# A Fourier mixing and gated feed-forward kernel: the order of six matmuls in a step of the tensor engine

## The chip, the cores and the metric

The kernel runs on one core of a Trainium2 chip. The core has a tensor engine for matrix products (PE in the profile; its loads of weights are PEld), a vector engine (DVE), a scalar engine (ACT), a general engine (POOL) and an engine that mostly issues transfers (SP). Matrix products land in PSUM, which DVE and ACT read; everything else lies in SBUF or in the chip's memory. Each engine works through its own list of instructions in order and waits on semaphores for the others. The metric is the device time of one execution, in microseconds (us), as the median of the runs made.

## The reference

```python
def _attn_ref(x):                       # x: (8, 3008, 256)
    X = np.fft.fft(x, axis=1)
    X = np.fft.fft(X, axis=2)
    return X.real.astype(np.float32)

def _moe_ref(x, w_gate, w_val, w_out):  # 24064 tokens, d_model 256, d_ff 1536
    gate = np.maximum(x @ w_gate, 0.0)
    val = x @ w_val
    return (gate * val @ w_out).astype(np.float32)

def reference(...):
    x = _attn_ref(x).reshape(24064, 256)
    return _moe_ref(x, w_gate, w_val, w_out)
```

The input is mixed by a Fourier transform along the sequence and the features, of which the real part is kept. Each token then goes through a gate (with a relu), a value, their product and an output projection.

## The kernel before, in words

The sequence transform of length 3008 is taken as 94 x 32, in two stages of matrix products with a trip through the chip's memory between them. For each of the eight batches, `stage1` (eight pieces, matmuls of L117 and L121) makes the first stage. `shuffle_out` (L134) and `shuffle_in` (L140) write its result out and read it back in another layout, both issued by SP. `rotate` (L146, L147) mends one column, and `stage2` (L157, six pieces) makes the tiles `pq`, one for each of three blocks of a batch. The feature transform is folded into the weights: `wc`, `ws` and `wm` hold gate (index 0) and value (index 1) weights multiplied by cosines and sines. Before stage 1, POOL folds the input of a batch (L88 to L100), which SP (L73) and POOL itself (L76, a gather) have loaded.

The transform of a real input has a mirror symmetry, and the feed-forward uses it. A block's tile `pq` has a part 0 and a part 1. For 128 of the 1536 hidden units at a time, one step computes the gate `G` and the value `V` for 512 tokens as `wc` times part 0 plus `ws` times part 1 (the function `plus`). ACT takes the relu of `G` into `gs` (L349) and DVE multiplies it with `V` into the first half of `h` (L350). Then the function `minus` adds one more product, `wm` times part 1, into the same `G` and `V`, which turns them into the gate and value of the 512 mirrored tokens. Again ACT takes a relu (L360) and DVE a product (L362, into the second half of `h`, with the tokens turned round). So the matmul of `minus` into `G` must wait until the relu of `plus` has read `G`, and the matmul of `minus` into `V` until the product of `plus` has read `V`.

There are 8 x 3 x 12 = 288 steps. The kernel's order is written out by hand: instructions go to each engine in the order of the code. The main loop makes one turn for each step and twelve more. Turn t does `minus` of step t-1, `plus` of step t, then what the table `extra` holds for this turn (the pieces of the coming batch: `load_x`, `fold_all`, `stage1`, the two shuffles, `rotate`, `stage2`), and then `out_piece` of step t-12, eight matmuls with the output weights (L380). The first twelve turns have no output matmuls, and the last twelve have nothing else. Every third turn an output tile `po` is complete; it is copied by DVE (L384) and by ACT (L386) in turn, at the end of the turn that completes it, and after each copy by ACT four stores are issued on SP (L395 or L401). For the second batch, stage 1 falls in turns 16 to 23, the shuffles are issued in turn 24 and `rotate` stands in turn 28; for later batches eight turns of stage 1 end one turn before the shuffles, and `rotate` comes seven turns after these.

`G` and `V` have two PSUM buffers each, `gs` has four, `h` has 25.

Of the kernel before, what the change touches and what calls it, by code (L numbers as in the profile page):

```python
# [10 lines left out]
F32 = mybir.dt.float32  # L11
BF16 = mybir.dt.bfloat16
I32 = mybir.dt.int32
ALU = mybir.AluOpType
ACTF = mybir.ActivationFunctionType
# [10 lines left out]
def free(ap, offset, *dims):  # L26

    part = list(ap.ap[0])
    return bass.AP(ap.tensor, ap.offset + offset, [part] + [list(d) for d in dims])
# [12 lines left out]
def kernel(ctx: ExitStack, tc, x, w_gate, w_val, w_out, out):  # L42
# [3 lines left out]
    nc = tc.nc  # L46
    B, S, D = x.shape
    DF = w_gate.shape[1]
    NA, NB = 94, 32
# [125 lines left out]
    wc = [const.tile([128, DF], BF16, tag=f"wc{i}", name=f"wc{i}") for i in range(2)]  # L175
    ws = [const.tile([128, DF], BF16, tag=f"ws{i}", name=f"ws{i}") for i in range(2)]
    wm = [const.tile([128, DF], BF16, tag=f"wm{i}", name=f"wm{i}") for i in range(2)]
    wo = const.tile([128, NF, D], BF16, tag="wo")

    with tc.tile_pool(name="st", bufs=1, space=SB) as st, \  # L180
# [3 lines left out]
        for i, w in enumerate((w_gate, w_val)):  # L184
            t = st.tile([128, 2, DF], F32, tag=f"wst{i}", name=f"wst{i}")
# [122 lines left out]
        for n in range(DF // 512):  # L308
            for i in range(2):
                for cs in range(2):  # L310
                    ps = psw.tile([128, 512], F32, tag="w", name="psw")
                    for c in range(2):
                        nc.tensor.matmul(ps[:], lhsT=cd[:, c, cs, :], rhs=wst[i][:, c, n * 512:(n + 1) * 512],  # L313
                                         start=(c == 0), stop=(c == 1))
# [13 lines left out]
    gp = ctx.enter_context(tc.tile_pool(name="gp", bufs=4, space=SB))  # L328
    hp = ctx.enter_context(tc.tile_pool(name="hp", bufs=2 * NF + 1, space=SB))
    op = ctx.enter_context(tc.tile_pool(name="op", bufs=4, space=SB))  # L330
    psg = ctx.enter_context(tc.tile_pool(name="psg", bufs=2, space=PS))
    psv = ctx.enter_context(tc.tile_pool(name="psv", bufs=2, space=PS))
    pso = ctx.enter_context(tc.tile_pool(name="pso", bufs=2, space=PS))

    steps = [(b, blk, f) for b in range(B) for blk in range(NBLK) for f in range(NF)]
    ht = {}

    def plus(b, blk, f):
        pq = pqt[b, blk]
        fs = slice(f * 128, (f + 1) * 128)  # L340
        h = hp.tile([128, 2, 512], BF16, tag="h", name="h")
        G = psg.tile([128, 512], F32, tag="g", name="G")
        V = psv.tile([128, 512], F32, tag="v", name="V")
        ht[b, blk, f] = (h, G, V)
        for i, acc in enumerate((G, V)):
            nc.tensor.matmul(acc[:], lhsT=wc[i][:, fs], rhs=pq[:, 0, :], start=True, stop=False)  # L346
            nc.tensor.matmul(acc[:], lhsT=ws[i][:, fs], rhs=pq[:, 1, :], start=False, stop=True)  # L347
        gs = gp.tile([128, 512], F32, tag="gs", name="gs")
        nc.scalar.activation(gs[:], G[:], ACTF.Relu)  # L349
        nc.vector.tensor_tensor(h[:, 0, :], gs[:], V[:], op=ALU.mult)  # L350

    def minus(b, blk, f):
        pq = pqt[b, blk]
        fs = slice(f * 128, (f + 1) * 128)
        h, G, V = ht[b, blk, f]
        for i, acc in enumerate((G, V)):
            nc.tensor.matmul(acc[:], lhsT=wm[i][:, fs], rhs=pq[:, 1, :], start=False, stop=True,  # L357
                             skip_group_check=True)
        gs = gp.tile([128, 512], F32, tag="gs", name="gs")
        nc.scalar.activation(gs[:], G[:], ACTF.Relu)  # L360

        nc.vector.tensor_tensor(free(h[:], 512 + NB - 1, [NB, 16], [-1, NB]),  # L362
                                gs[:].rearrange("p (a k) -> p a k", k=NB),
                                V[:].rearrange("p (a k) -> p a k", k=NB), op=ALU.mult)
        ht[b, blk, f] = h

    state = {}

    def out_piece(b, blk, f):

        for k in range(8 * f, 8 * f + 8):
            gi, ff = divmod(k, NF)
            sg, s = divmod(gi, 4)
            g = 3 - s if sg else s
            if s == 0 and ff == 0:
                state["os"] = op.tile([128, 4, D], F32, tag="os", name="os")
            if s % 2 == 0 and ff == 0:
                state["po"] = pso.tile([128, 2, D], F32, tag="o", name="po")
            po, os_ = state["po"], state["os"]
            nc.tensor.matmul(po[:, s % 2, :], lhsT=ht[b, blk, ff][:, sg, g * 128:(g + 1) * 128],  # L380
                             rhs=wo[:, ff, :], start=(ff == 0), stop=(ff == NF - 1))
            if s % 2 == 1 and ff == NF - 1:
                if s == 1:
                    nc.vector.tensor_copy(os_[:, s - 1:s + 1, :], po[:])  # L384
                else:
                    nc.scalar.copy(os_[:, s - 1:s + 1, :], po[:])  # L386
            if s == 3 and ff == NF - 1:
                store(b, blk, sg, os_)
# [35 lines left out]

    n = len(steps)
    for t in range(n + NF):
        if 0 < t <= n:
            minus(*steps[t - 1])
        if t < n:
            plus(*steps[t])  # L430
        for fn in extra.get(t, ()):
            fn()
        if t >= NF:
            b, blk, f = steps[t - NF]
            out_piece(b, blk, f)
# [30 lines left out]
```

## Time and profile before

| | us |
|---|---|
| median of 3 runs | 752.11 |
| lowest and highest | 751.88, 752.16 |
| the profiled execution | 752.15 |
| its span in the profile | 750.4 |
| first matmul of the main loop starts (in the span) | 70.87 |
| first output matmul starts | 98.42 |
| last matmul that isn't an output matmul starts | 734.21 |

How to read it: the profiled execution is one run with the hardware profiler on, and its span goes from the first to the last instruction that the profile shows, so that some 1.75 us of its time lie around the span. Times within the profile are counted from the span's start. The page of the profile gives each engine's busy time, the granted clock of the tensor engine in slices, the groups of instructions by line of the code, and which instruction ended each wait. The timeline gives single instructions: start, duration, engine, line, operation, tiles written and read, and in brackets the idle time of that engine before the instruction with the engine and line that ended it. The end of a matmul is modelled, and matmuls overlap: of two that follow each other without a wait, the second starts before the row of the first has ended. Buffer numbers stand behind the names of tiles where several tiles have one name.

### The profile page before, as it was taken

Reading aid. Unit: us, or ns where it says so; the run is one execution under the profiler, and the core shown is the slowest. Engines: PE = TensorE matmul, PEld = TensorE weight load, DVE = VectorE, ACT = ScalarE, POOL = GpSimd, SP = SyncE. Lnnn points to the kernel's source line nnn. Section 1 sums busy time; section 2 is a strip of 40 time slices with the busy share of each in tenths; the row PEclk is TensorE's granted clock in tenths of the full one; section 3 lists DMA queues with packets and bytes.
Section 4 is the critical chain, followed back from the end, with each engine's and each line's share of the span. In section 5 each row is a group of like instructions: output and inputs, shape, how many; then the busy total and the mean of one; then the engine's idle time right before and its main releaser. Section 6 shows DMA issues by size and latency. Waiting matters only on the chain.

```text
span 750.4 us, 12199 instructions
## 1 busy us (share of the span) xinstructions
PE 692.4 (92%) x4432; PEld 430.6 (57%) x4432; DVE 481.0 (64%) x747; ACT 408.3 (54%) x701; POOL 221.6 (30%) x116
## 2 busy tenths in 40 slices
PE   0178799999999999999999999999999999999997
PEld 0033256566666666666666666666666666666565
DVE  6613666666666766766666767666667667666672
ACT  2114556556565656556565655556565655555551
POOL 2837739102920086004900094005800000000000
PEclk9999999999999999999999999999999999999999
DMA  9466253616342534116241454135221141211213
GB/s 195 165 164 113 62 112 93 157 29 151 104 111 57 115 112 113 56 41 172 71 135 33 116 139 111 29 82 143 59 55 29 32 136 28 53 33 28 55 29 82
DMA packets 26971, 67.61 MB, mean 90 GB/s; under 512 B 3856, under 2 KB 17680, under 8 KB 24720
## 3 DMA queue, kind: packets, MB, share of 16 engines
q1 hardware_dynamic: 24340, 51.84, 26.6%
q0 software_dynamic: 2448, 13.37, 8.2%
q10 hardware_dynamic: 124, 1.64, 0.9%
q8 instruction: 34, 0.56, 0.3%
q14 instruction: 25, 0.20, 0.1%
HBM read 36.68 MB, written 30.93 MB: 90 GB/s over the span
## 4 chain that ended last, share of the span: by engine, by line
PE 82%; DVE 6%; ACT 4%; POOL 3%; issue 3%; DMA 1%; ACTq 0%; POOLq 0%; DVEq 0%
PE po L380 30%; PE V L357 10%; PE G L347 7%; PE G L346 7%; PE V L347 7%; PE V L346 7%; PE G L357 7%; DVE h L350 4%; PE psw L313 3%; ACT gs L360 2%; ACT gs L349 1%; DVE h L362 1%; DMA t_969<-Td 1%; DMA Td<-t_719 1%; DVE q L37 0%
## 5 line engine op out<-in xcount | busy, mean ns | idle before, releaser
L362 DVE TENSOR_TENSOR h<-gs,V 128x512 bf16<-128x512 f32 x288 | 198.1, 688 | 203.4 <-ACT gs L360 148.6
L380 PE MATMUL po<-wo,h 128*128 128x256 bf16 x2304 | 296.8, 272 | 0.0
L360 ACT ACTIVATE gs<-G 128x512 f32<-128x512 f32 x288 | 172.2, 598 | 214.1 <-PE G L357 214.1
L380 PEld LDWEIGHTS <-h 128*128 128x128 bf16 x2304 | 222.7, 98 | 64.1 <-issue 2.0
L350 DVE TENSOR_TENSOR h<-gs,V 128x512 bf16<-128x512 f32 x288 | 197.8, 687 | 11.3 <-ACT gs L349 9.9
L349 ACT ACTIVATE gs<-G 128x512 f32<-128x512 f32 x288 | 172.3, 598 | 30.9 <-PE G L347 14.7
L88 POOL TENSOR_TENSOR xc<-xl,xh 94x3840 f32<-94x3840 f32 (+1 forms) x8 | 60.6, 7574 | 302.2 <-DMA xl<-in_x_dram 268.8
L357 PE MATMUL V<-pq,wm_92 128*128 128x512 bf16 x288 | 108.6, 377 | 6.3 <-DVE h L350 4.2
L357 PE MATMUL G<-pq,wm_91 128*128 128x512 bf16 x288 | 109.1, 379 | 3.1 <-ACT gs L349 3.1
L347 PE MATMUL V<-pq,ws_90 128*128 128x512 bf16 x288 | 109.2, 379 | 0.0
L346 PE MATMUL V<-pq,wc_88 128*128 128x512 bf16 x288 | 109.0, 378 | 0.0
L347 PE MATMUL G<-pq,ws_89 128*128 128x512 bf16 x288 | 108.9, 378 | 0.0
L346 PE MATMUL G<-pq,wc_87 128*128 128x512 bf16 x288 | 108.8, 378 | 0.0
L89 POOL TENSOR_TENSOR xl<-xl,xh 94x3840 f32<-94x3840 f32 (+1 forms) x8 | 60.6, 7578 | 0.6
L346 PEld LDWEIGHTS <-wc_87 128*128 128x128 bf16 x288 | 27.7, 96 | 54.5 <-issue 43.2
L347 PEld LDWEIGHTS <-ws_90 128*128 128x128 bf16 x288 | 28.0, 97 | 34.2
L386 ACT COPY os<-po 128x512 f32<-128x512 f32 x48 | 28.1, 586 | 35.6 <-PE po L380 35.6
L346 PEld LDWEIGHTS <-wc_88 128*128 128x128 bf16 x288 | 27.8, 97 | 34.3
L347 PEld LDWEIGHTS <-ws_89 128*128 128x128 bf16 x288 | 27.7, 96 | 34.2
L117 PEld LDWEIGHTS <-w_82 94*96 94x96 bf16 x120 | 15.7, 131 | 50.5 <-issue 28.1
L384 DVE COPY os<-po 128x512 f32<-128x512 f32 x48 | 33.0, 688 | 6.9 <-PE po L380 6.9
L357 PEld LDWEIGHTS <-wm_92 128*128 128x128 bf16 x288 | 28.2, 98 | 9.6 <-issue 6.5
(345 smaller groups left out, 346.8 us busy)
## 6 DMA issues: line engine op xcount, KB each, us to landing
out_dram<-os SPq DMA_DIRECT2D x176, 128.0 KB, 2.1
xl<-in_x_dram SPq DMA_DIRECT2D x7, 1360.0 KB, 9.8
xl<-in_x_dram SPq DMA_DIRECT2D x7, 238.0 KB
wst_103<-in_moe_w_gate_dram SPq DMA_DIRECT2D x2, 768.0 KB, 20.4
wst_106<-in_moe_w_val_dram SPq DMA_DIRECT2D x2, 768.0 KB, 23.7
out_dram<-os SPq DMA_DIRECT2D x16, 96.0 KB, 4.5
xl<-in_x_dram ACTq DMA_DIRECT2D x1, 1360.0 KB
Td<-t_256 SPq DMA_DIRECT2D x4, 192.0 KB, 9.2
```

Of the source, the lines that this page charges most:

```text
L88: eng.tensor_tensor(c1, x1, rev, op=ALU.subtract)
L89: eng.tensor_tensor(x1, x1, rev, op=ALU.add)
L346: nc.tensor.matmul(acc[:], lhsT=wc[i][:, fs], rhs=pq[:, 0, :], start=True, stop=False)
L347: nc.tensor.matmul(acc[:], lhsT=ws[i][:, fs], rhs=pq[:, 1, :], start=False, stop=True)
L349: nc.scalar.activation(gs[:], G[:], ACTF.Relu)
L350: nc.vector.tensor_tensor(h[:, 0, :], gs[:], V[:], op=ALU.mult)
L357: nc.tensor.matmul(acc[:], lhsT=wm[i][:, fs], rhs=pq[:, 1, :], start=False, stop=True, skip_group_check=True)
L360: nc.scalar.activation(gs[:], G[:], ACTF.Relu)
L362: nc.vector.tensor_tensor(free(h[:], 512 + NB - 1, [NB, 16], [-1, NB]), gs[:].rearrange("p (a k) -> p a k", k=NB), V[:].rearrange("p (a k) ...
L380: nc.tensor.matmul(po[:, s % 2, :], lhsT=ht[b, blk, ff][:, sg, g * 128:(g + 1) * 128], rhs=wo[:, ff, :], start=(ff == 0), stop=(ff == NF - 1))
L384: nc.vector.tensor_copy(os_[:, s - 1:s + 1, :], po[:])
L386: nc.scalar.copy(os_[:, s - 1:s + 1, :], po[:])
```

## The change

`plus` and `minus` get a further argument, 0 for the gate and 1 for the value, and do only that half. The main loop runs over it, so that a turn's matmuls come as: `minus` into G, `plus` into G (two), `minus` into V, `plus` into V (two). Before, both matmuls of `minus` came first.

```diff
-    def plus(b, blk, f):
+    def plus(b, blk, f, i):
...
-        for i, acc in enumerate((G, V)):
-            nc.tensor.matmul(acc[:], lhsT=wc[i][:, fs], rhs=pq[:, 0, :], start=True, stop=False)
-            nc.tensor.matmul(acc[:], lhsT=ws[i][:, fs], rhs=pq[:, 1, :], start=False, stop=True)
-        gs = gp.tile([128, 512], F32, tag="gs", name="gs")
-        nc.scalar.activation(gs[:], G[:], ACTF.Relu)
-        nc.vector.tensor_tensor(h[:, 0, :], gs[:], V[:], op=ALU.mult)
...
+        e = ht[b, blk, f]
+        nc.tensor.matmul(e[i][:], lhsT=wc[i][:, fs], rhs=pq[:, 0, :], start=True, stop=False)
+        nc.tensor.matmul(e[i][:], lhsT=ws[i][:, fs], rhs=pq[:, 1, :], start=False, stop=True)
+        if i == 0:
+            e["gs"] = gp.tile([128, 512], F32, tag="gs", name="gs")
+            nc.scalar.activation(e["gs"][:], e[0][:], ACTF.Relu)
+        else:
+            nc.vector.tensor_tensor(e["h"][:, 0, :], e["gs"][:], e[1][:], op=ALU.mult)
...
     for t in range(n + NF):
-        if 0 < t <= n:
-            minus(*steps[t - 1])
-        if t < n:
-            plus(*steps[t])
+        for i in range(2):
+            if 0 < t <= n:
+                minus(*steps[t - 1], i)
+            if t < n:
+                plus(*steps[t], i)
         for fn in extra.get(t, ()):
             fn()
```

`minus` is split in the same way: its one matmul by `i`, the relu with the gate, the product with the value. Each engine keeps the number of its instructions. ACT's and DVE's lists stay in their order (relu of `minus`, relu of `plus`; product of `minus`, product of `plus`), and so do the lists of SP and POOL. The change moves lines of the code: L346, L347 and L357 before are L347, L348 and L360 after; the relus L349 and L360 are L351 and L364, the products L350 and L362 are L353 and L367, the output matmuls L380 are L385.

The tensor engine's list at the first turn with a `minus` (turn 1; V_435 and G_434 are tiles of step 0, V_450 and G_449 before, V_448 and G_447 after, those of step 1; in brackets the semaphore that an instruction waits for, by the engine that raises it). Before:

```order
L357 LDWEIGHTS wm0_91
L357 MATMUL G_434<-pq_376,wm0_91 128x512 [waits Activation_49]
L357 LDWEIGHTS wm1_92
L357 MATMUL V_435<-pq_376,wm1_92 128x512 [waits DVE_49]
L346 LDWEIGHTS wc0_87
L346 MATMUL G_449<-pq_376,wc0_87 128x512
L347 LDWEIGHTS ws0_89
L347 MATMUL G_449<-pq_376,ws0_89 128x512
L346 LDWEIGHTS wc1_88
L346 MATMUL V_450<-pq_376,wc1_88 128x512
```

The same place after:

```order
L360 LDWEIGHTS wm0_91
L360 MATMUL G_434<-pq_376,wm0_91 128x512 [waits Activation_49]
L347 LDWEIGHTS wc0_87
L347 MATMUL G_447<-pq_376,wc0_87 128x512
L348 LDWEIGHTS ws0_89
L348 MATMUL G_447<-pq_376,ws0_89 128x512
L360 LDWEIGHTS wm1_92
L360 MATMUL V_435<-pq_376,wm1_92 128x512 [waits DVE_49]
L347 LDWEIGHTS wc1_88
L347 MATMUL V_448<-pq_376,wc1_88 128x512
```

The matmul of `minus` into V, with its wait for DVE and its load of weights, has moved behind the two matmuls of `plus` into G, and now stands right ahead of the matmuls of `plus` into V.

A turn with output matmuls and a piece of stage 1 (buffer numbers left out). Before:

```order
L380 MATMUL po<-wo,h 128x256
L357 LDWEIGHTS wm_91
L357 MATMUL G<-pq,wm_91 128x512 [waits Activation_49]
L357 LDWEIGHTS wm_92
L357 MATMUL V<-pq,wm_92 128x512 [waits DVE_49]
L346 LDWEIGHTS wc_87
L346 MATMUL G<-pq,wc_87 128x512
L347 LDWEIGHTS ws_89
L347 MATMUL G<-pq,ws_89 128x512
L346 LDWEIGHTS wc_88
L346 MATMUL V<-pq,wc_88 128x512 [waits PE_49]
```

And after:

```order
L385 MATMUL po<-wo,h 128x256
L360 LDWEIGHTS wm_91
L360 MATMUL G<-pq,wm_91 128x512 [waits Activation_49]
L347 LDWEIGHTS wc_87
L347 MATMUL G<-pq,wc_87 128x512
L348 LDWEIGHTS ws_89
L348 MATMUL G<-pq,ws_89 128x512
L360 LDWEIGHTS wm_92
L360 MATMUL V<-pq,wm_92 128x512 [waits DVE_49]
L347 LDWEIGHTS wc_88
L347 MATMUL V<-pq,wc_88 128x512 [waits PE_49]
```

The move is the same. From turn 2 on, the first matmul of `plus` into V waits for a semaphore that PE itself raises. That wait stands at the same matmul in both kernels; the matmul of `minus` into V was three matmuls ahead of it and is now next to it.

More of the change, by code (lines that the diff above doesn't have):

```diff
@@ L336 @@
     ht = {}
-    def plus(b, blk, f):
+    def plus(b, blk, f, i):
         pq = pqt[b, blk]
         fs = slice(f * 128, (f + 1) * 128)
[L341 to L344, printed above, removed]
-        for i, acc in enumerate((G, V)):
-            nc.tensor.matmul(acc[:], lhsT=wc[i][:, fs], rhs=pq[:, 0, :], start=True, stop=False)
-            nc.tensor.matmul(acc[:], lhsT=ws[i][:, fs], rhs=pq[:, 1, :], start=False, stop=True)
-        gs = gp.tile([128, 512], F32, tag="gs", name="gs")
-        nc.scalar.activation(gs[:], G[:], ACTF.Relu)
-        nc.vector.tensor_tensor(h[:, 0, :], gs[:], V[:], op=ALU.mult)
@@ L352, in minus @@
-    def minus(b, blk, f):
+        if i == 0:
+            ht[b, blk, f] = {"h": hp.tile([128, 2, 512], BF16, tag="h", name="h"),
+                             0: psg.tile([128, 512], F32, tag="g", name="G"),
+                             1: psv.tile([128, 512], F32, tag="v", name="V")}
+        e = ht[b, blk, f]
+        nc.tensor.matmul(e[i][:], lhsT=wc[i][:, fs], rhs=pq[:, 0, :], start=True, stop=False)
+        nc.tensor.matmul(e[i][:], lhsT=ws[i][:, fs], rhs=pq[:, 1, :], start=False, stop=True)
@@ L353, in minus @@
+        if i == 0:
+            e["gs"] = gp.tile([128, 512], F32, tag="gs", name="gs")
+            nc.scalar.activation(e["gs"][:], e[0][:], ACTF.Relu)
+        else:
+            nc.vector.tensor_tensor(e["h"][:, 0, :], e["gs"][:], e[1][:], op=ALU.mult)
+    def minus(b, blk, f, i):
         pq = pqt[b, blk]
         fs = slice(f * 128, (f + 1) * 128)
[L355 to L365, printed above, removed]
+        e = ht[b, blk, f]
+        nc.tensor.matmul(e[i][:], lhsT=wm[i][:, fs], rhs=pq[:, 1, :], start=False, stop=True,
+                         skip_group_check=True)
@@ L367 @@
+        if i == 0:
+            e["gs"] = gp.tile([128, 512], F32, tag="gs", name="gs")
+            nc.scalar.activation(e["gs"][:], e[0][:], ACTF.Relu)
+        else:
+            nc.vector.tensor_tensor(free(e["h"][:], 512 + NB - 1, [NB, 16], [-1, NB]),
+                                    e["gs"][:].rearrange("p (a k) -> p a k", k=NB),
+                                    e[1][:].rearrange("p (a k) -> p a k", k=NB), op=ALU.mult)
+            ht[b, blk, f] = e["h"]
     state = {}
```

## The prediction

> **What bounds the kernel now.** I read the page's engine totals first.
>
> ```profile
> span 750.4 us, 12199 instructions
> PE 692.4 (92%) x4432; PEld 430.6 (57%) x4432; DVE 481.0 (64%) x747; ACT 408.3 (54%) x701; POOL 221.6 (30%) x116
> PEclk9999999999999999999999999999999999999999
> PE V L357 <- DVE h L350: 4.2, 12, 0.4
> PE G L357 <- ACT gs L349: 3.1, 12, 0.3
> ```
>
> PE is busy 92% of the span at its full granted clock (the tenths of the page are all 9). The last two rows are from the list of waits: PE waits for the product of L350 and the relu of L349, 7.3 us in all, in 12 turns. That undercounts, because a matmul row lasts 0.38 us and the next one starts 0.216 us after it: a late start of up to 0.16 us hides under the row before. So the rest is read from start times in the timeline, and I call a turn's work m.G, m.V (L357), p.G, p.V (L346 and L347, two each), relu m (L360), relu p (L349), product m (L362), product p (L350) and outs (eight of L380).
>
> One of the first twelve turns, which have no outs yet (start, duration, engine, line; in brackets the idle time before):
>
> ```profile
> 72.98 0.38 PE L357 MATMUL V<-pq,wm_92 128*128 128x512 bf16 x1 [0.40 <-DVE h L350]
> 73.46 0.69 DVE L362 TENSOR_TENSOR h<-gs,V 128x512 bf16<-128x512 f32 x1 [0.54 <-PE V L357]
> ...
> 75.19 0.38 PE L357 MATMUL V<-pq,wm_92 128*128 128x512 bf16 x1 [0.35 <-DVE h L350]
> 75.41 0.38 PE L346 MATMUL G<-pq,wc_87 128*128 128x512 bf16 x1
> 75.62 0.38 PE L347 MATMUL G<-pq,ws_89 128*128 128x512 bf16 x1
> ...
> 76.04 0.60 ACT L349 ACTIVATE gs<-G 128x512 f32<-128x512 f32 x1 [0.56 <-PE G L347]
> ...
> 76.67 0.69 DVE L350 TENSOR_TENSOR h<-gs,V 128x512 bf16<-128x512 f32 x1 [0.30 <-ACT gs L349]
> 76.69 0.38 PE L357 MATMUL G<-pq,wm_91 128*128 128x512 bf16 x1 [0.25 <-ACT gs L349]
> ...
> 77.41 0.38 PE L357 MATMUL V<-pq,wm_92 128*128 128x512 bf16 x1 [0.34 <-DVE h L350]
> ```
>
> The turn is a ring: m.V 75.19, second p.G 75.62, relu p 76.04, product p 76.67, m.V 77.41. That is 2.22 us, though six matmuls 0.216 apart need 1.29. The delays to reuse: matmul start to ACT start 0.42 (75.62 to 76.04), matmul start to DVE start 0.48 (72.98 to 73.46), relu start to product start 0.63, relu start to matmul 0.65 (76.04 to 76.69), product start to matmul 0.74 (76.67 to 77.41).
>
> A turn with outs, late in the run:
>
> ```profile
> 657.75 0.38 PE L357 MATMUL G<-pq,wm_91 128*128 128x512 bf16 x1
> 658.02 0.38 PE L357 MATMUL V<-pq,wm_92 128*128 128x512 bf16 x1
> ...
> 659.09 1.04 PE L380 MATMUL po<-wo,h 128*128 128x256 bf16 x8
> 659.49 0.69 DVE L350 TENSOR_TENSOR h<-gs,V 128x512 bf16<-128x512 f32 x1
> ...
> 659.97 0.38 PE L357 MATMUL G<-pq,wm_91 128*128 128x512 bf16 x1
> 660.24 0.38 PE L357 MATMUL V<-pq,wm_92 128*128 128x512 bf16 x1
> ```
>
> m.V starts 0.27 after m.G instead of 0.216, and 0.74 or 0.75 after product p (659.49): it still waits for that product, by 0.05. Outs take 0.88 (659.09 to 659.97), so 0.88 + 1.29 = 2.17 would do where the turn takes 2.22. Where a copy of an output sits on ACT, the wait is larger:
>
> ```profile
> 125.47 0.59 ACT L386 COPY os<-po 128x512 f32<-128x512 f32 x1 [0.29 <-PE po L380]
> 125.95 0.60 ACT L360 ACTIVATE gs<-G 128x512 f32<-128x512 f32 x1
> 126.44 0.60 ACT L349 ACTIVATE gs<-G 128x512 f32<-128x512 f32 x1
> 126.59 0.69 DVE L362 TENSOR_TENSOR h<-gs,V 128x512 bf16<-128x512 f32 x1 [1.33 <-ACT gs L360]
> 127.19 0.68 DVE L350 TENSOR_TENSOR h<-gs,V 128x512 bf16<-128x512 f32 x1
> ...
> 127.44 0.38 PE L357 MATMUL G<-pq,wm_91 128*128 128x512 bf16 x1
> 127.93 0.38 PE L357 MATMUL V<-pq,wm_92 128*128 128x512 bf16 x1
> ```
>
> Here m.V comes 0.49 after m.G, so PE loses 0.27. The rows also price operations that are queued back to back: DVE starts one 0.60 after the other (126.59, 127.19), ACT 0.49 (125.95, 126.44).
>
> Taking the m.G and m.V starts of all 288 turns, first and last with outs being
>
> ```profile
> 99.29 0.38 PE L357 MATMUL G<-pq,wm_91 128*128 128x512 bf16 x1
> 99.56 0.38 PE L357 MATMUL V<-pq,wm_92 128*128 128x512 bf16 x1
> ...
> 733.95 0.38 PE L357 MATMUL G<-pq,wm_91 128*128 128x512 bf16 x1
> 734.21 0.38 PE L357 MATMUL V<-pq,wm_92 128*128 128x512 bf16 x1
> ```
>
> I count 276 turns with outs: 155 lose 0.05 (7.8 us), 27 lose 0.21 to 0.28 (6.5 us), 6 lose 0.02 or 0.03 (0.15 us), 88 nothing. Together **14.4 us**: 0.3 in the first twelve of them, 0.65 in the next four, 13.45 after.
>
> **The change part by part.** No instruction is added or removed. Each turn's m.V goes behind two matmuls of p.G, 0.43 us later; DVE, ACT, the DMA queues keep their order. So three things have to be worked out.
>
> *First twelve turns.* The ring no longer runs through p.G and relu p. With m.V at 0: product m at 0.48, product p behind it at 0.48 + 0.60 = 1.08 (p.V, second start at 0.43, would allow 0.91), next m.V at 1.08 + 0.74 = 1.82. The relus fit: this turn's m.G came at 0.65 - 1.82 = -1.17, relu m at -0.75, relu p 0.49 behind it at -0.26, so the next m.G may go at 0.39, and PE is free for it at 0.65. Eleven rounds from 72.98 put the twelfth m.V at 72.98 + 20.0 = 93.0 and, with only p.V behind it, outs at 93.65. Now they start here:
>
> ```profile
> 97.34 0.38 PE L357 MATMUL V<-pq,wm_92 128*128 128x512 bf16 x1 [0.35 <-DVE h L350]
> ...
> 98.42 1.04 PE L380 MATMUL po<-wo,h 128*128 128x256 bf16 x8
> ```
>
> The gain is 98.42 - 93.65 = **4.8 us**. The one uncertain price is the 0.60 between two products. [...]
>
> *Turns with outs.* With m.G at 0: relu m 0.42; p.G 0.22 and 0.43; relu p at 0.91; m.V 0.65; product m 1.13; p.V 0.86 and 1.08; product p at 1.73; outs 1.29 to 2.17; the next m.V at 2.82. It needs product p by 1.73 + 0.74 = 2.47: **0.35 to spare**, where 0.05 was short. Behind an ACT copy relu m starts at 0.69 instead of 0.42, product m at 1.32, product p at 1.92, ready at 2.66: 0.16 to spare. A DVE copy starts about 0.2 into the next turn, behind product p, and frees DVE 0.60 later at 0.8, before product m at 1.13. Thus all 14.4 us vanish from PE's order; nothing is late next but PE itself. What queues behind a waiting m.V is p.V and the outs, as before p.G.
>
> *One place takes some back.* At turn 28 PE waits for data that went out and came in by DMA:
>
> ```profile
> 127.90 0.36 SPq L134 DMA_DIRECT2D Td<-t_719  x1
> 132.32 0.38 SPq L140 DMA_DIRECT2D t_969<-Td  x1
> 132.89 0.94 POOL L76 DMA_INDIRECT xh<-in_x_dram,ix  x1
> ...
> 137.64 0.18 PE L146 MATMUL psr<-t_969,rot 128*128 128x12 bf16 x1 [1.60 <-DMA t_969<-Td]
> ```
>
> The DMA out is issued on SP behind four stores that wait for the copy at 125.47, that is for PE's turn 23. So the 4.8 + 0.3 us of the turns before pass through it, while the 0.65 us of turns 24 to 27 are only waited longer: they count 0. The way back takes 5.3 us (132.32 to 137.6) and meets the gather that POOL issues at 132.89, which hangs on no matmul of these turns; 5 us earlier it would miss it. What the view of the tile says of this transfer and of those of two later blocks (time to landing):
>
> ```profile
> DMA to landing us min/median/max: 5.3/5.3/5.3
> ...
> DMA to landing us min/median/max: 5.0/5.0/5.0
> ...
> DMA to landing us min/median/max: 4.8/4.8/4.8
> ```
>
> I take 5.0, a gain of 0.3 us; 4.8 is the better bound, and as much lost, 0.5, the worse. Later blocks leave seven turns between transfer and use, and wait nowhere.
>
> **Sum.** 4.8 + 0.3 + 0 + 0.3 + 13.45 = 18.85 us. The profiled execution took 752.15 us (span 750.4 and 1.75 around it), 0.04 above the median of the three runs, 752.11. 752.15 - 18.85 = **733.3 us**, 2.5% less.
>
> **The rivals.**
>
> *The gap is not the wait for product p.* If the 0.05 belonged to m.V's weights, it would move along, and only the first turns would gain: 752.15 - 4.8 - 0.3 = 747. Against it: 88 turns load the same weights and lose nothing, and in the rows of 127.93 and 660.24 m.V follows product p by the same 0.74. 2%.
>
> *The early gain is waited out.* If the transfer of turn 28 hung on something that PE does not move, the 4.8 + 0.3 us and the 0.3 would go and 13.45 remain: 738.7. Against it stands the copy of 125.47 ahead of it, which waits for PE. 4%.
>
> *Part of the wait stays.* If products come late in turns with copies by more than the 0.16 worked out, up to the 6.5 us of the 27 large waits remain: 734 to 740. 8%.
>
> *Slower: p.V waits for the m.V next to it.* The order shows a wait for PE's own semaphore on the first p.V. Today that matmul comes 0.65 after m.V and a wait for m.V could hide; moved to 0.216 behind it, it would show from 0.216 on. With the 0.48 that a matmul's end takes to reach DVE as price, each turn would lose 0.26: 276 x 0.26 = 72 us, 752.15 - 18.85 + 72 = 805 us. Against it: V has two buffers, so the owner of p.V's buffer is the tile two steps back, whose last matmul ran a whole turn earlier. 3%.
>
> **How the numbers follow.** Forecast 80%, its rivals 17% as above, 3% for no visible change, by causes I do not see. A measurement of this kernel can tell about 0.2% (1.5 us) from no change. The forecast's own bounds: 0.69 for the spacing adds 1.0, the transfer 0.2 to 0.8, and some turns may keep a small wait, 2 to 3 us; below, a ring shorter than 1.82 saves at most a few us more. That is 731 to 736.5; with the third rival's lower half, the range is 731 to 737.5. Faster by over 0.2%: 0.94; within: 0.03; slower: 0.03.
>
> **What would show it.** Right: turns of 1.82 us before the first outs, those at about 93.7; m.V 0.216 behind p.G and turns without other work 2.17 us long, with nothing on top; the wait at turn 28 grown from 1.8 to about 2; product m and product p 0.60 apart. Wrong: m.V rows with a late start after outs began (third rival), p.V late (slower), a first turn of 1.9 or more (the spacing), or the wait at turn 28 grown by 5 us.

## The result and the profile after

| | before | after |
|---|---|---|
| median, us | 752.13 (4 runs) | 734.73 (4 runs) |
| lowest and highest, us | 751.88, 754.24 | 734.03, 735.44 |
| the profiled execution, us | 752.15 | 735.31 |
| its span, us | 750.4 | 733.5 |
| first output matmul starts, us | 98.42 | 93.32 |
| last matmul that isn't an output matmul starts, us | 734.21 | 717.39 |

The ratio of after to before is 0.9763, 95% interval 0.9741 to 0.9784. The kernel is 17.4 us faster by the medians; 18.85 were forecast. Over all sessions the kernel before was timed 47 times: 35 executions lie between 751.2 and 753.5 us, seven between 754.2 and 754.6 and five between 761.1 and 762.0 at mean clocks of 0.989 to 0.991, and none of these twelve slower ones was profiled.

From the page and the list of waits of the changed kernel (busy time of an engine and its share of the span; who waited for whom, total, times, longest):

```profile
span 733.5 us, 12121 instructions
PE 676.0 (92%) x4354; PEld 432.3 (59%) x4432; DVE 462.5 (63%) x747; ACT 381.8 (52%) x701; POOL 221.5 (30%) x116
PE V L360 <- DVE h L353: 3.9, 11, 0.4
PE psr L146 <- DMA t_969<-Td: 2.0, 1, 2.0
```

PE's share is 92% as before, although waits are gone: busy time counts modelled rows of 0.38 us that overlap (starts 0.22 apart) and cover small waits, so it can't show this change. (78 matmul records are missing here, hence x4354.) The 11 waits that are left belong to the first turns. One of these in the timeline after (m.V is now L360, product m L367, product p L353, and p.V L347 and L348):

```profile
76.28 0.38 PE L360 MATMUL V<-pq,wm_92 128*128 128x512 bf16 x1 [0.37 <-DVE h L353]
...
76.77 0.69 DVE L367 TENSOR_TENSOR h<-gs,V 128x512 bf16<-128x512 f32 x1 [0.54 <-PE V L360]
...
77.37 0.68 DVE L353 TENSOR_TENSOR h<-gs,V 128x512 bf16<-128x512 f32 x1
...
78.10 0.38 PE L360 MATMUL V<-pq,wm_92 128*128 128x512 bf16 x1 [0.37 <-DVE h L353]
...
93.32 1.03 PE L385 MATMUL po<-wo,h 128*128 128x256 bf16 x8
```

The ring is m.V, product m, product p, m.V: 0.49, 0.60, 0.73, in all 1.82 us. The second product starts while the row of the first has 0.09 to run. A late turn after:

```profile
642.48 1.04 PE L385 MATMUL po<-wo,h 128*128 128x256 bf16 x8
642.93 0.68 DVE L353 TENSOR_TENSOR h<-gs,V 128x512 bf16<-128x512 f32 x1
643.36 0.38 PE L360 MATMUL G<-pq,wm_91 128*128 128x512 bf16 x1
643.57 0.38 PE L347 MATMUL G<-pq,wc_87 128*128 128x512 bf16 x1
...
643.79 0.38 PE L348 MATMUL G<-pq,ws_89 128*128 128x512 bf16 x1
644.00 0.38 PE L360 MATMUL V<-pq,wm_92 128*128 128x512 bf16 x1
644.22 0.38 PE L347 MATMUL V<-pq,wc_88 128*128 128x512 bf16 x1
```

Each matmul comes 0.21 or 0.22 after the one before, m.V and the p.V next to it too. Product p starts at 642.93, so m.V could come at 643.67; its place is 644.00, 0.33 later. No matmul waits.

What the forecast had not seen stands at turn 28. The timeline after, and the windows of 1 us there (per engine the busy time and count; PEclk is the granted clock, then DMA share and GB/s):

```profile
120.14 0.58 ACT L391 COPY os<-po 128x512 f32<-128x512 f32 x1 [0.29 <-PE po L385]
...
122.56 0.37 SPq L134 DMA_DIRECT2D Td<-t_719  x1
126.97 0.38 SPq L140 DMA_DIRECT2D t_969<-Td  x1
...
132.02 0.18 PE L146 MATMUL psr<-t_969,rot 128*128 128x12 bf16 x1 [1.95 <-DMA t_969<-Td]
...
134.46 0.63 PE L360 MATMUL V<-pq,wm_92 128*128 128x512 bf16 x1
134.89 0.63 PE L347 MATMUL V<-pq,wc_88 128*128 128x512 bf16 x1
```

```profile
131.00:132.00 1.00, 0.00 (x0) 0.00 (x0) 0.03 (x1) 0.00 (x0) 1.00 (x2) 1.00 0.13 32
132.00:133.00 1.00, 0.98 (x9) 0.79 (x9) 0.21 (x1) 0.00 (x0) 0.85 (x3) 0.82 0.00 0
133.00:134.00 1.00, 0.81 (x3) 0.41 (x3) 0.00 (x0) 0.15 (x1) 0.47 (x1) 0.50 0.00 0
134.00:135.00 1.00, 0.96 (x3) 0.40 (x3) 0.00 (x0) 0.74 (x2) 0.00 (x0) 0.50 1.15 246
135.00:136.00 1.00, 1.00 (x6) 0.44 (x5) 0.69 (x1) 0.30 (x1) 0.00 (x0) 0.50 0.94 279
136.00:137.00 1.00, 1.00 (x13) 0.91 (x11) 0.69 (x1) 0.58 (x1) 0.00 (x0) 0.97 1.05 246
```

Just after PE resumes from its wait of 1.95 us, the granted clock is half for about 3.4 us (0.36 of a us in the second row, three whole ones, 0.06 in the last), and matmuls come 0.43 apart (134.46 to 134.89). In the profile of before the wait was 1.6 us by the list of waits and no such stretch followed: the clock is 1.00 in its windows from 136 to 148 us.

Where the 16.9 us between the two spans came from, by the starts of the same matmuls in both traces:

| stretch | before | after | gain | forecast |
|---|---|---|---|---|
| span's start to the second p.G of turn 0 | 71.08 | 70.75 | 0.3 | 0 |
| to the first output matmul | 27.34 | 22.57 | 4.8 | 4.8 |
| to rotate of turn 28 | 39.22 | 38.70 | 0.5 | 0.6 |
| to m.G of turn 30 | 3.29 | 4.97 | -1.7 | 0 |
| to the last m.G | 593.02 | 580.10 | 12.9 | 13.45 |
| to the end of the span | 16.4 | 16.4 | 0 | 0 |

### The profile page after: what moved, and what is told of

It reads as the page before. It is cut to its first block, busy times and chain, and to the rows that moved or that the text cites. A ratio compares the mean times of both kernels' runs of the same rounds, so it can differ in the third digit from the quotient of the medians.

```text
span 733.5 us, 12121 instructions
## 1 busy us (share of the span) xinstructions
PE 676.0 (92%) x4354; PEld 432.3 (59%) x4432; DVE 462.5 (63%) x747; ACT 381.8 (52%) x701; POOL 221.5 (30%) x116
## 4 chain that ended last, share of the span: by engine, by line
PE 87%; DMA 4%; POOL 3%; DVE 3%; issue 1%; ACT 1%; SPq 0%; POOLq 0%; ACTq 0%; DVEq 0%
PE po L385 34%; PE G L348 9%; PE V L360 9%; PE G L360 8%; PE V L347 8%; PE V L348 8%; PE G L347 7%; DMA Td<-t_256 2%; DVE h L353 1%; DMA t_969<-Td 1%; DMA t_304<-Td 1%; DMA Td<-t_719 1%; DVE q L37 0%; POOL xl L89 0%; POOL q L35 0%
## 5 line engine op out<-in xcount | busy, mean ns | idle before, releaser
L367 DVE TENSOR_TENSOR h<-gs,V 128x512 bf16<-128x512 f32 x288 | 197.9, 687 | 215.5 <-PE V L360 161.2
L364 ACT ACTIVATE gs<-G 128x512 f32<-128x512 f32 x288 | 172.2, 598 | 242.0 <-PE G L360 242.0
L385 PE MATMUL po<-wo,h 128*128 128x256 bf16 x2304 | 297.1, 273 | 0.4
L385 PEld LDWEIGHTS <-h 128*128 128x128 bf16 x2304 | 222.8, 98 | 64.5 <-issue 2.4
L353 DVE TENSOR_TENSOR h<-gs,V 128x512 bf16<-128x512 f32 x288 | 195.9, 680 | 1.1 <-ACT gs L351 0.5
L351 ACT ACTIVATE gs<-G 128x512 f32<-128x512 f32 x288 | 171.1, 594 | 0.8 <-PE G L348 0.8
L360 PE MATMUL V<-pq,wm_92 128*128 128x512 bf16 x288 | 109.4, 380 | 4.2 <-DVE h L353 3.9
L348 PE MATMUL G<-pq,ws_89 128*128 128x512 bf16 x282 | 107.1, 380 | 2.9 <-issue 0.2
L360 PE MATMUL G<-pq,wm_91 128*128 128x512 bf16 x288 | 109.4, 380 | 0.4 <-ACT gs L351 0.3
L347 PE MATMUL V<-pq,wc_88 128*128 128x512 bf16 x288 | 109.4, 380 | 0.0
L348 PE MATMUL V<-pq,ws_90 128*128 128x512 bf16 x267 | 101.4, 380 | 0.0
L347 PE MATMUL G<-pq,wc_87 128*128 128x512 bf16 x237 | 89.8, 379 | 0.0
L347 PEld LDWEIGHTS <-wc_88 128*128 128x128 bf16 x288 | 28.2, 98 | 40.0 <-issue 7.5
L348 PEld LDWEIGHTS <-ws_90 128*128 128x128 bf16 x288 | 28.2, 98 | 34.2 <-issue 0.3
L348 PEld LDWEIGHTS <-ws_89 128*128 128x128 bf16 x288 | 28.2, 98 | 34.0 <-issue 0.3
L360 PEld LDWEIGHTS <-wm_92 128*128 128x128 bf16 x288 | 28.2, 98 | 34.0 <-issue 0.3
L347 PEld LDWEIGHTS <-wc_87 128*128 128x128 bf16 x288 | 28.2, 98 | 5.2 <-issue 0.8
```

The lines of the kernel that those rows point to most:

```text
L347: nc.tensor.matmul(e[i][:], lhsT=wc[i][:, fs], rhs=pq[:, 0, :], start=True, stop=False)
L348: nc.tensor.matmul(e[i][:], lhsT=ws[i][:, fs], rhs=pq[:, 1, :], start=False, stop=True)
L351: nc.scalar.activation(e["gs"][:], e[0][:], ACTF.Relu)
L353: nc.vector.tensor_tensor(e["h"][:, 0, :], e["gs"][:], e[1][:], op=ALU.mult)
L360: nc.tensor.matmul(e[i][:], lhsT=wm[i][:, fs], rhs=pq[:, 1, :], start=False, stop=True, skip_group_check=True)
L364: nc.scalar.activation(e["gs"][:], e[0][:], ACTF.Relu)
```

## The experiments

Theory A: a turn's m.V has a due time, 0.74 us after the start of product p; only lateness against it costs time, each turn for itself, and behind the wait of turn 28 some executions have the half clock. Each run below was timed beside runs of the kernel before.

**Once more.** The changed kernel as it is.

> The changed kernel, once more. Theory A: its executions differ by a stretch at half clock behind the 2.1 us wait of turn 28: about 734.1 us where the mean granted clock is 0.999 or 1.000, about 735.4 us where it is 0.997 or 0.998, and nothing between. Rival B (the spread has nothing to do with the clock): times and clocks are not paired like this.

Median 735.38 us (6 runs), ratio 0.9757 (0.9717 to 0.9796). With the four runs above there are ten executions, with their mean granted clock:

```
733.60 0.999   734.03 0.999   734.13 1.000   734.16 1.000
735.27 0.998   735.31 0.998   735.44 0.997   735.49 0.996   735.51 0.998   736.05 0.996
```

Two groups, means 733.98 and 735.51, and no time between. Two of the six slower executions were profiled (735.31 and 735.51), both at a mean clock of 0.998; the first is the one whose windows stand above, with 3.4 us at half clock behind the wait of turn 28. That the other five have such a stretch and the four faster ones lack it is inferred from times and mean clocks. Read so, the half clock costs 1.5 us and came in six of ten, as theory A says, except that two mean clocks are 0.996, below the 0.997 it gave.

**Rotate later.** The wait itself is taken away: two more turns lie between transfer and use.

```diff
-        tl, t1, tr, t2, d2 = (17, 16, 28, 29, 1) if b == 0 else (10, 4, 19, 20, 2)
+        tl, t1, tr, t2, d2 = (17, 16, 30, 31, 1) if b == 0 else (10, 4, 19, 20, 2)
```

> The changed order, and for the second batch rotate in turn 30 instead of 28 and the six stage-2 pieces in turns 31 to 36. Theory A: PE reaches rotate 4.3 us later than now and finds its data landed, so the 2.1 us wait and the half clock behind it are gone: 734.1 - 2.1 = 732.0 us in all executions, mean clock 0.999 or more in all. Rival B (the half clock comes whatever PE waits for): executions at 0.997 or 0.998 remain, some 1.3 us above the others. Rival C (the wait only moves to another place): 734 to 735.4 us as now.

Median 731.64 us, 731.34 to 732.38, ratio 0.9716 (0.9677 to 0.9755); 3.7 us under the changed kernel in the same session, and 2.3 under the four executions above that seem to have no half clock. The clock stays full where it had dropped, by the window of this kernel:

```profile
132.00:136.00 4.00, 4.00 (x29) 2.54 (x27) 2.39 (x5) 2.30 (x6) 1.23 (x3) 1.00 0.49 127
```

The time is as theory A says, and rivals B and C fall; theory A's sentence on the mean clock is not right, since two executions read 0.998. One of these two is the profiled one, and its clock is 1.00 in the windows from 128 to 140 us. The mean also counts the time behind the last matmul, where the clock can be lower: in the profile of before it is 1.00 up to 748.4 us and 0.50 from 749 on, with no matmul there. So the mean shows a half-clock stretch only together with the time. This is the fastest version of the study.

**Rotate earlier.** The opposite: the wait is made longer.

```diff
-        tl, t1, tr, t2, d2 = (17, 16, 28, 29, 1) if b == 0 else (10, 4, 19, 20, 2)
+        tl, t1, tr, t2, d2 = (17, 16, 27, 29, 1) if b == 0 else (10, 4, 19, 20, 2)
```

> The changed order, with rotate in turn 27 instead of 28, so that PE waits there 2.17 us longer, about 4.3 us, for the same data. Theory A (a wait of over 2 us brings the half clock, for 3.4 us): every execution has it, 734.1 + 2.2 + 1.4 = 737.7 us, and none lies near 736.3. Rival B (the half clock comes by itself, in some executions): two groups, near 736.3 and 737.7 us, as now.

Median 738.07 us, 737.67 to 739.1, ratio 0.9784 (0.9735 to 0.9833), one group, mean clocks 0.994 to 0.996. In the profiled execution the wait was 4.5 us. From its list of waits, and its windows of 4 us, in which the granted clock is the third number from the right:

```profile
PE psr L146 <- DMA t<-Td: 4.8, 2, 4.5
...
128.00:132.00 4.00, 0.00 (x0) 0.00 (x0) 0.76 (x2) 0.00 (x0) 4.00 (x4) 0.73 0.71 197
132.00:136.00 4.00, 3.81 (x14) 1.94 (x14) 0.31 (x2) 1.19 (x2) 1.37 (x3) 0.50 0.52 131
136.00:140.00 4.00, 3.95 (x28) 2.70 (x28) 2.55 (x4) 1.67 (x3) 0.00 (x0) 0.91 1.11 254
```

The clock is 0.73, 0.50 and 0.91, which makes 2.2 + 4.0 + 0.7 = 6.9 us at half clock, twice the stretch of the changed kernel, where the expectation had one; its first part falls into the wait itself. So here the drop comes with the wait (mean clocks of 0.994 to 0.996 in all six executions), and not by itself.

**The old order with rotate later.**

```diff
-        tl, t1, tr, t2, d2 = (17, 16, 28, 29, 1) if b == 0 else (10, 4, 19, 20, 2)
+        tl, t1, tr, t2, d2 = (17, 16, 30, 31, 1) if b == 0 else (10, 4, 19, 20, 2)
...
-        for i in range(2):
-            if 0 < t <= n:
+        pairs = [(minus, 0), (plus, 0), (minus, 1), (plus, 1)] if False else \
+            [(minus, 0), (minus, 1), (plus, 0), (plus, 1)]
+        for fn, i in pairs:
+            if fn is minus and 0 < t <= n:
                 minus(*steps[t - 1], i)
-            if t < n:
+            if fn is plus and t < n:
                 plus(*steps[t], i)
```

The condition is `False`, so every turn has the old order.

> The old order of the matmuls, with rotate in turn 30 and stage 2 in turns 31 to 36. Theory A (the wait of turn 28 was there before the change, 1.8 us without half clock, and two turns more, 4.4 us, cover it): 752.1 - 1.8 = 750.3 us; moving rotate is worth about 1.3 us less than with the new order, where the wait was 2.1 us and some executions had the half clock behind it. Rival (the wait is a product of the new order alone): 752.1 us.

Median 750.54 us (12 runs) against 752.35, a gain of 1.8 us as theory A says. The ratio's interval, 0.9981 (0.9945 to 1.0017), reaches 1, so by the times alone the gain isn't clear of the noise: three executions lay near 757 at a mean clock of 0.994, and their cause is open. In the profile the wait of turn 28 no longer stands in the list of waits, and the span is 748.7 us against 750.4. By the medians, rotate later is worth about 1.9 us more with the new order than with the old.

**The new order in the first turns alone, and in the later ones alone.**

```diff
-        for i in range(2):
-            if 0 < t <= n:
-                minus(*steps[t - 1], i)
-            if t < n:
-                plus(*steps[t], i)
+        pairs = [(minus, 0), (plus, 0), (minus, 1), (plus, 1)] if t <= NF else \
+            [(minus, 0), (minus, 1), (plus, 0), (plus, 1)]
+        for fn, i in pairs:
+            if fn is minus and 0 < t <= n:
+                minus(*steps[t - 1], i)
+            if fn is plus and t < n:
+                plus(*steps[t], i)
```

The other kernel has `t > NF` in the condition.

> The new order in turns 0 to 12 alone, the old order after. Theory A (the gain is the wait of the mirror value matmul for the product, in each turn for itself): 752.1 - 4.8 - 0.3 = 747.0 us, the turns before the first output matmuls 1.82 us long, the later ones 2.22 us as before. Rival D (the gain of the later turns comes from the early start, which takes DVE's products out of PE's way for good): near 735 us.

> The old order in turns 0 to 12, the new order from turn 13 on. Theory A: 752.1 - 0.3 - 12.9 = 738.9 us, up to 740.5 us where the wait of turn 28, then 2.4 us, brings the half clock; turns of 2.22 us before the first output matmuls, 2.17 us late in the run. Rival D: near 752 us. If it and first_turns_only together give less than the whole change (17.4 us of gain), the parts help each other.

The first gave 747.19 us (ratio 0.9922, 0.9897 to 0.9947), the second 739.98 us (ratio 0.982, 0.978 to 0.986), between 738.38 and 741.02. Two places in the timeline of the first kernel:

```profile
81.58 0.38 PE L360 MATMUL V<-pq,wm 128*128 128x512 bf16 x1 [0.37 <-DVE h L353]
...
83.40 0.38 PE L360 MATMUL V<-pq,wm 128*128 128x512 bf16 x1 [0.37 <-DVE h L353]
...
652.18 0.38 PE L360 MATMUL G<-pq,wm 128*128 128x512 bf16 x1
652.45 0.38 PE L360 MATMUL V<-pq,wm 128*128 128x512 bf16 x1
...
654.40 0.38 PE L360 MATMUL G<-pq,wm 128*128 128x512 bf16 x1
```

The early turns are 1.82 us, the late ones 2.22 us with m.V 0.27 behind m.G, as in the kernel before. The early start gives the later turns nothing, so rival D falls. Gains of 5.2 and 12.4 us make 17.5, against 17.0 for the whole change in the same session: within the spread of the runs the parts add up. The second kernel shows the wait of turn 28 at 2.5 us in its list of waits, and a mean clock of 0.997 in its profile.

**m.V only half as far.** It goes behind one matmul of p.G, not two; `between` is the value's half of `minus` in the call for the gate, and nothing in the call for the value.

```diff
-    def plus(b, blk, f, i):
+    def plus(b, blk, f, i, between=lambda: None):
...
         nc.tensor.matmul(e[i][:], lhsT=wc[i][:, fs], rhs=pq[:, 0, :], start=True, stop=False)
+        between()
         nc.tensor.matmul(e[i][:], lhsT=ws[i][:, fs], rhs=pq[:, 1, :], start=False, stop=True)
...
```

> The mirror value matmul behind the first of the two matmuls of plus into G, not behind both. Theory A (each m.V has a due time, product p plus 0.74 us, and only lateness against it costs): in turns with outs m.V comes at 0.43 of the turn, product p at 1.70 is ready at 2.44 for the next m.V at 2.60, so plain turns stay 2.17 us; behind an ACT copy product p is ready at 2.66, 0.06 late, 27 times, 1.6 us in all. In the first turns relu p now follows m.V, and the ring is m.V, second p.G, relu p, product p: 0.22 + 0.42 + 0.63 + 0.74 = 2.01 us, 0.19 longer, 2.1 us in all. Together 734.1 to 735.4 plus 3.7: 738 to 739 us. Rival D (it only matters that m.V isn't right behind m.G): 734 to 735.5 us.

Median 737.73 us (4 runs), ratio 0.9785 (0.972 to 0.985); three executions lie at 737.6 to 737.8, just under the 738 to 739 expected, and one at 739.71. The first turns are 2.0 us long. A turn behind an ACT copy, in this kernel's timeline (product p is L354):

```profile
654.31 0.59 ACT L392 COPY os<-po 128x512 f32<-128x512 f32 x1 [0.71 <-PE po L386]
...
656.04 0.68 DVE L354 TENSOR_TENSOR h<-gs,V 128x512 bf16<-128x512 f32 x1
...
656.28 0.38 PE L361 MATMUL G<-pq,wm 128*128 128x512 bf16 x1
...
656.77 0.38 PE L361 MATMUL V<-pq,wm 128*128 128x512 bf16 x1
```

m.V comes 0.73 after product p and 0.49 after m.G, where 0.43 is its place: 0.06 late. By the starts of all turns, 25 of the turns behind an ACT copy are 0.05 longer than in the changed kernel, and all other late turns but one, and those around the wait of turn 28, are the same. The due time of m.V, not merely its distance from m.G, sets what is lost.

**The spare time used up.** DVE gets one product more in each turn, whose result nobody reads.

```diff
...
+            sc = scp.tile([128, 256], BF16, tag="sc", name="sc")
+            nc.vector.tensor_tensor(sc[:], e["gs"][:, 0:256], e[1][:, 0:256], op=ALU.mult)
             nc.vector.tensor_tensor(e["h"][:, 0, :], e["gs"][:], e[1][:], op=ALU.mult)
```

The second kernel has 512 in place of 256.

> The changed order, and in each turn DVE multiplies the first 256 columns of the gate and value of plus a second time, into a tile that nobody reads, ahead of product p. By the rows of 128x256 and 128x512 (425 and 688 ns) the added operation takes 0.60 - 0.26 = 0.34 us of DVE. Theory A: plain turns had 0.35 us to spare and stay 2.17 us; the 27 turns behind an ACT copy had 0.16 and lose 0.18 each, 4.9 us; the first turns grow from 1.82 to 2.16 us, 3.7 us. Together 743 to 744 us. Rival E (DVE has room: it is busy 63% and the operation is hidden): 734 to 735.5 us.

> The same with all 512 columns, 0.60 us more of DVE ahead of product p. Theory A: the 0.35 us to spare is used up, each of the 178 plain turns loses 0.25 (44 us), the 98 turns with a piece of stage 1 or 2 or rotate, 0.22 longer, lose 0.03 (3 us), the 27 behind an ACT copy 0.19 more (5 us), the first twelve 0.60 (6.6 us): 734.5 + 59 = 793 us; PE's wait for product p is back in the list of its waits or in late starts of m.V. Rival E: under 740 us, since DVE would be busy some 85%.

The half product gave 746.81 us (ratio 0.9894, 0.9829 to 0.9959), the whole one 807.47 us in its one execution. Rival E falls: DVE was busy 63% before the addition, and still has no room for 0.60 us more ahead of product p. The timeline of the whole one (the added product is L355, product p L356):

```profile
693.45 0.68 DVE L355 TENSOR_TENSOR sc<-gs,V 128x512 bf16<-128x512 f32 x1
693.88 0.38 PE L363 MATMUL G<-pq,wm 128*128 128x512 bf16 x1
694.04 0.68 DVE L356 TENSOR_TENSOR h<-gs,V 128x512 bf16<-128x512 f32 x1
...
694.78 0.38 PE L363 MATMUL V<-pq,wm 128*128 128x512 bf16 x1
...
696.29 0.38 PE L363 MATMUL G<-pq,wm 128*128 128x512 bf16 x1
```

m.V comes 0.74 after product p and 0.90 after m.G, where 0.65 is its place. The turn is 2.41 us, 0.24 over the changed kernel's 2.17, where 0.25 was worked out. With the half product plain turns stay at 2.17, 25 of those behind an ACT copy are 0.17 longer (0.18 was expected for 27) and the first ones 0.33 longer. The totals were missed by some 3 and 14 us: the expectations had left out the turns behind a DVE copy, which stands in DVE's list ahead of product m. In the profile of the half product 16 of the 45 late turns that follow a DVE copy are 0.09 to 0.34 us longer, 3.1 us in all. With the whole product the wait of turn 28 also grew, to 6.7 us. By the starts of m.G in the two traces, turns 28 and 29 took 6.0 us more than in the changed kernel, for which the expectation had nothing. The 45 turns behind a DVE copy took 18.0 us more; had they been ordinary turns, 18 without other work and 27 with a piece of stage 1 or 2, the expectation's 0.25 and 0.03 would give 5.3.

## Why the prediction was right

- **What bounds it.** Right. PE's late starts at m.V were the time to be had, and the wait for product p was their cause: the first-turns and later-turns kernels lose or keep them turn by turn, and each kernel that made product p later by a known amount made m.V later by what was left over.
- **The first twelve turns.** 4.8 us forecast, 4.8 measured; the ring is 1.82 us. DVE's spacing of 0.60, the one uncertain price, is seen in each of these turns (76.77 to 77.37). In the trace product p starts 0.59 to 0.61 behind product m in 281 of the 286 places where it follows without a wait. The forecast's worse bound took 0.69, the length of the row; no turn before the first outs shows that spacing.
- **Turns with outs.** Forecast 13.45 us behind turn 28, measured 12.9. All late starts went, as the starts of m.G and m.V show for every later turn. The rest is of the size of the rounding: a turn that lost 0.05 by its starts became 0.047 us shorter (2.216 to 2.169). The 0.35 us to spare is 0.33 in the trace.
- **Turn 28.** The early gain did pass through the transfer, and the wait grew. The transfer took 5.0 us instead of 5.3, as taken. The step that was mis-sized is "I take 5.0, a gain of 0.3 us; 4.8 is the better bound, and as much lost, 0.5, the worse": the wait was priced at its own length alone, and the half clock behind it cost 1.7 us more in the profiled execution, outside that bound. The four faster executions have a mean of 734.0, 0.7 over the forecast.
- **The rivals.** The gap that moves with the weights, the early gain waited out, and part of the wait staying: none occurred in the changed kernel (747, 738.7 and up to 740 us were their times). The slower one neither: p.V follows m.V by 0.22 us (644.00 to 644.22), so its wait for PE's own semaphore is for an earlier matmul.

## What to carry to other kernels

A matmul that is modelled as longer than its issue interval (here 0.38 us and 0.22) hides late starts: compare start times with the interval before calling an engine fully used. In a fixed order, work out for each waiting instruction when what it waits for is ready, and put work that waits for nothing in front of the ones that are late; how busy the other engine is says little about it (DVE was busy 64% before). A single wait of the tensor engine can cost more than its length: here one of 1.95 us was followed by 3.4 us at half clock, and two turns more between transfer and use brought 3.7 us. So a transfer deserves a turn or two more of distance than its own time asks for.

## What the runs showed of the hardware

A wait of 2.0 us was followed by about 3.4 us at half clock in the profiled execution, and by the times and mean clocks in six of ten executions, at 1.5 us each; with a wait of 4.5 us the clock was half for 6.9 us, from within the wait on. Where the wait of the profiled execution was 2.13 us (half a move), one execution of four has a mean clock of 0.997 and three 0.999; where it was 2.6 us (half a product), the four have 0.996, 0.997, 0.999 and 0.999. Theory A's "a wait of over 2 us brings the half clock" doesn't hold everywhere, and length alone doesn't decide: in the profile of half a move a longer wait than the changed kernel's is followed by full clock (the third number from the right in the windows).

```profile
134.75 0.18 PE L146 MATMUL psr<-t,rot 128*128 128x12 bf16 x1 [2.13 <-DMA t<-Td]
...
130.00:134.00 4.00, 2.50 (x15) 1.46 (x15) 2.73 (x4) 1.79 (x3) 3.35 (x6) 1.00 0.70 199
134.00:138.00 4.00, 3.25 (x27) 2.37 (x27) 1.52 (x3) 1.78 (x3) 0.00 (x0) 1.00 1.05 238
```

What makes one wait bring the half clock and another not is not shown by these runs.

Product p mostly follows product m on DVE at 0.60 us (76.77 to 77.37 after), and relu p follows relu m on ACT at 0.49 us (125.95 to 126.44 before) where neither waits, though their rows are 0.69 and 0.60 us long.
